# A chunked recurrence feeding two expert layers: one join product moved from TensorE to VectorE, three logits products, a Gram product placed later, and new values as sixteen wider products

## The chip, the cores and the metric

The kernel runs on one core of a Trainium2 chip. The time is the device time of one execution in microseconds (us), from the core's first to its last instruction with what lies around it. The engines are TensorE (PE; its weight loads are shown apart as PEld), VectorE (DVE), ScalarE (ACT), GpSimd (POOL) and SyncE (SP, which here only issues transfers). Each runs its own instructions in program order and waits on semaphores for the others.

## What is computed

The reference is a recurrence over 768 steps for 4 x 8 heads of 40 x 40 state, followed by a routed expert layer (8 experts, one per token) and a dense layer of 2048 hidden units:

```python
for t in range(S):
    y[:, :, t] = np.einsum('bhd,bhde->bhe', rt, state)
    Sa = np.einsum('bhde,bhe->bhd', state, at)
    state_decay = state * wt[:, :, None, :] - np.einsum('bhd,bhe->bhde', Sa, bt)
    state = state_decay + np.einsum('bhd,bhe->bhde', vt, kt)
# then x = y as (3072 tokens, 320)
expert_idx = np.argmax(x @ w_gate, axis=1)          # capacity 768 per expert
out[i] = gate_w[i] * (relu(x_i @ w1[e]) @ w2[e])
return relu(out @ w_in) ** 2 @ w_out
```

All of it is float32. The change touches the recurrence and the gate alone.

## The kernel before

The recurrence is cut into 24 chunks of 32 steps. Inside a chunk the steps depend on each other through a strictly lower triangular 32 x 32 matrix for each of the 32 heads; the kernel inverts it, so that a chunk becomes a set of small matrix products, and carries the 40 x 40 states from chunk to chunk. Four chunks' inverses are built together ("a group"): `inv_start` turns the group's matrices (`GM`) into `L` with a VectorE transpose and lists fifteen jobs, each an elementwise product into `pr` and a reduction (lines 278 and 279). Seven jobs substitute forward through 8 x 8 blocks, four (`left`, into `Xm`) and four (`right`) join pairs of 8 x 8 blocks to 16 x 16 ones. `inv_end` transposes the result into `TT` and `nat` (lines 344 and 345). The last join, of two 16 x 16 blocks to 32 x 32, is on TensorE for each chunk: `join` (32 products, line 315), a ScalarE copy to `jm` (line 318), `join_end` (32 products, line 330) and four ScalarE copies into the block matrix `TB` (`join_out`, line 340).

The loop in `run` (line 678) goes over the chunks c = 1 to 22; m is c modulo 4. All engines' order is the order of the calls. In an iteration TensorE does: `u(c)` (new values, line 442), `solve(c + 1)` (line 428), `gram(c + 7)` (line 204), `nat_k(c + 1)` with `y(c - 1)` inside it (lines 382 and 538), the gate's `logits` (line 873), `vu_t(c)` (line 504), `state(c)` (line 460), `join(c + 2)`, `scores(c)` (line 516), `nat_a(c + 2)` (line 382), `join_end(c + 2)`, in some iterations `count` (line 911), `gate.xT` (line 857) and `state_t(c + 1)` (line 487). A float32 product is two TensorE records, each a weight load and a matmul; a transpose is one. VectorE does the scans of chunk c + 8 (lines 159 and 163), the Gram mask (line 219), `gate_in` (line 547), `state_decay` (line 472 for even c, 475 for odd), the scores' mask (line 524) and, by the table `PLAN`, the inverse jobs: eight at the end of m = 0, three and fifteen (all that are left, and `inv_end`) in m = 1. ScalarE copies nearly every result out of PSUM and issues a share of the loads; GpSimd scales chunk c + 8 (`scale`, line 187) and copies the diagonal blocks (`block_T`, line 354).

PSUM tiles come from two double banks that alternate (`big`) and four single banks (`bank`): each new tile waits until the readers of the one before it in its place are done. `load_w` (line 146) brings one of the decay arrays of a chunk into the buffer `wB`, on SyncE's queue; with three buffers in turn it waits for `scale` of an earlier chunk. Ahead of the loop stands a prologue for chunks 0 to 8, written out by hand; after it come the last chunk and the expert and dense layers.

Of the kernel before, what the change touches and what calls it, by code (L numbers as in the profile page):

```python
# [35 lines left out]
class Attention:  # L36
# [8 lines left out]
    def __init__(self, tc, es, gate, zt, eb, E, VN, VR, R0, R1, x, ident):  # L45
# [45 lines left out]
        self.nat = self.natb.rearrange("p (a s) -> p a s", s=16)  # L91
        self.st, self.nb = {}, 0
# [114 lines left out]
    def gram_mask(self, c, first=True):  # L207
# [4 lines left out]
        nn = self.p2.tile([128, 2, 4, 32], F32, tag="N", name=f"N{c}", bufs=7)  # L212
# [10 lines left out]
    def inv_start(self, gi, mulengine):  # L223
# [16 lines left out]
        def left(base, xo, h, c0, c1, j0, k):  # L240
            jobs.append((gr, mulengine(k, h), ap(self.Xm, xo + c0 * h, [[h, c1 - c0], [1, h]]),
# [8 lines left out]
        for ms, h in (((0, 1), 8),):  # L250
            k = 0
            for i in range(0, h, 4):
                for g in ms:
                    st = 4 if 4 * h * (h - i) <= 640 else 2
                    for c in range(i, i + 4, st):
                        left(g * 2 * h * 33, g * 64, h, c, c + st, c, k)
                        k += 1
            gr += 1
            for i in reversed(range(0, h, 4)):
                for g in ms:  # L260
                    st = 4 if 4 * h * (i + 4) <= 640 else 2
                    for r in range(i, i + 4, st):
                        right(g * 2 * h * 33, g * 64, h, r, r + st, r + st, k)
                        k += 1
            gr += 1
        self.iv = (gi, jobs, {}, [0, 0])

    def inv(self, n):
# [5 lines left out]
        for k in range(pos[0], min(pos[0] + n, len(jobs))):  # L274
            _, _, out, in0, in1, shape = jobs[k]
            pr = self.p2.tile([128, 256], F32, tag="prod1", name=f"pr{gi}_{k}", bufs=1)
# [3 lines left out]
            pos[0] = k + 1  # L280
        if pos[0] == len(jobs):
            self.inv_end()

    def inv_blocks(self):
# [3 lines left out]
        own, other = self.GM[1].rearrange("p a b -> p (a b)"), self.natb  # L288
        prods, k, n = {}, 0, [0, 0]
        for i in range(len(jobs)):  # L290
            while k < len(jobs) and k <= i + 2 and jobs[k][0] == jobs[i][0]:
                _, eng, out, in0, in1, shape = jobs[k]
                z = eng is not V
# [13 lines left out]
    def join(self, c):  # L307

        if c >= NC:
            return  # L310
# [1394 lines left out]
```

## Time and profile before

| | us |
|---|---|
| median of 3 runs | 1085.13 (1077.47 to 1091.61) |
| the profiled execution's own time | 1090.35 |
| its span, first to last instruction | 1088.6 |
| the loop's iterations c = 1 to 16, by the first matmuls of `u` | 77.58 to 351.55 |
| the loop's iterations c = 17 to 22 | 351.55 to 439.50 |

The profile is of one execution. A row of instruction groups gives the line, the engine, the operation, the tiles, the shapes and the count, then the busy time in us and the mean duration of one in ns. "Idle before" is the time in which the engine stood still just ahead of the instruction, with what ended it; "issue" means that no wait that the profile shows ended it.

### The profile page before, as it was taken

What the parts mean: (1) busy time and instruction counts of PE and PEld (TensorE: products, weight loads), DVE (VectorE), ACT (ScalarE), POOL (GpSimd) and SP (SyncE); (2) the same over time, 40 slices, a digit from 0 to 9 for tenths busy, and PEclk for the clock granted to TensorE, in tenths of its full rate; (3) what the DMA queues carried; (4) which work ended last, traced back from release to release, by engine and by line L of the source; (5) the groups of instructions that cost most, each with busy time, mean ns of one, the idle gap of its engine ahead of it and who ended that gap; (6) DMA issues with size and microseconds to landing.
All of it is one profiled execution on the core that took longest, in us unless ns stands there. A gap on an engine that the chain in (4) does not pass through costs nothing.

```text
span 1088.6 us, 36815 instructions
## 1 busy us (share of the span) xinstructions
PE 958.5 (88%) x15578; PEld 864.7 (79%) x15578; DVE 667.5 (61%) x1368; ACT 567.1 (52%) x1342; POOL 336.6 (31%) x531
## 2 busy tenths in 40 slices
PE   5378888977888899788999998899999999999995
PEld 3367777866777888678988998789899998999995
DVE  6978566584665635747878888957534444444432
ACT  8246466565565677345655555456534343534332
POOL 5452354443554121115645555414301010000000
PEclk8588898998899889899999999899999999999998
DMA  7744655545442233274677666523100000000000
GB/s 186 184 115 145 209 156 160 160 124 177 116 138 90 66 119 101 69 200 146 190 228 216 218 213 201 166 73 105 49 25 25 25 26 25 1 25 1 26 1 27
DMA packets 80671, 123.10 MB, mean 113 GB/s; under 512 B 9679, under 2 KB 57409, under 8 KB 79561
## 3 DMA queue, kind: packets, MB, share of 16 engines
q1 hardware_dynamic: 71173, 100.09, 31.7%
q10 hardware_dynamic: 7020, 12.78, 4.1%
q0 software_dynamic: 2304, 7.78, 2.3%
q8 instruction: 124, 2.03, 0.8%
q14 instruction: 50, 0.41, 0.1%
HBM read 91.36 MB, written 29.35 MB: 111 GB/s over the span
## 4 chain that ended last, share of the span: by engine, by line
PE 71%; issue 7%; DMA 7%; DVE 7%; ACT 5%; SPq 1%; POOL 1%; ACTq 0%; DVEq 0%; POOLq 0%
PE phg L1368 16%; PE phe L1368 6%; PE pog L1394 5%; PE pog L1393 5%; PE pog L1392 5%; PE pq L516 4%; PE px L428 4%; DMA xs<-zs_s 3%; PE ps L460 3%; PE poe L1394 2%; PE poe L1392 2%; PE poe L1393 2%; DMA wB<-in_E_dram 2%; PE pa L382 2%; PE jl L315 2%
## 5 line engine op out<-in xcount | busy, mean ns | idle before, releaser
L1378 DVE SCALAR_TENSOR_TENSOR sqg<-phg,rg 128x512 f32<-128x512 f32 x96 | 66.3, 691 | 119.0 <-ACT rg L1377 119.0
L1377 ACT ACTIVATE rg<-phg 128x512 f32<-128x512 f32 x96 | 57.2, 596 | 110.4 <-PE phg L1368 110.2
L1380 DVE TENSOR_TENSOR hlg<-sqg,hhg 128x512 fp32r<-128x512 f32 x96 | 66.6, 693 | 65.9 <-ACT hhg L1379 63.2
L1379 ACT CAST hhg<-sqg 128x512 fp32r<-128x512 f32 x96 | 59.6, 620 | 78.5 <-DVE sqg L1378 78.5
L1368 PE MATMUL phg<-xhg,e 128*128 128x512 f32 x264 | 93.1, 393 | 0.0
L428 PE MATMUL px<-TB,X 128*104 128x128 f32 x384 | 60.8, 318 | 15.3 <-issue 14.1
L1394 PE MATMUL pog<-e,hlg 128*128 128x320 f32 x240 | 74.1, 309 | 0.0
L1393 PE MATMUL pog<-e,hhg 128*128 128x320 f32 x240 | 74.1, 309 | 0.0
L1392 PE MATMUL pog<-e,hhg 128*128 128x320 f32 x240 | 74.0, 308 | 0.0
L428 PEld LDWEIGHTS px<-TB,X 128*104 128x104 f32 x384 | 54.1, 203 | 17.9 <-issue 15.1
L1186 POOL TENSOR_TENSOR e<-rw,e 128x256 fp32r<-128x256 f32 x51 | 43.1, 848 | 72.2 <-ACT e L1185 69.1
L187 POOL TENSOR_TENSOR e<-e 104x512 f32<-104x512 f32 x21 | 27.9, 1327 | 121.2 <-DVE e L163 82.2
L187 POOL TENSOR_TENSOR e<-e,wB 104x512 f32<-104x512 f32 x41 | 54.0, 1337 | 35.7 <-DVE wB L159 17.1
L1507 POOL DMA_INDIRECT x2g<-zs_s,idx x24 | 23.7, 989 | 113.5 <-ACT hhg L1379 105.7
L1368 PE MATMUL phe<-xhe,e 128*128 128x480 f32 (+4 forms) x176 | 58.5, 373 | 0.0
L1368 PEld LDWEIGHTS phg<-xhg,e 128*128 128x128 f32 x264 | 49.6, 188 | 8.8
L1394 PE MATMUL poe<-e,hle 128*120 128x320 f32 (+4 forms) x150 | 47.8, 318 | 7.0 <-DVE hle L1373 7.0
L1372 ACT ACTIVATE hhe<-phe 128x480 fp32r<-128x480 f32 (+4 forms) x64 | 33.9, 530 | 36.0 <-PE phe L1368 35.7
L417 ACT ACTIVATE rhsY<-pk,sgn 64x640 f32<-64x640 f32 x48 | 38.0, 791 | 27.9 <-PE py L538 25.4
L1368 PE MATMUL phg<-xlg,e 128*128 128x512 f32 x132 | 51.7, 392 | 0.0
L354 POOL COPY TB<-TT 32x256 f32<-32x256 f32 x92 | 39.6, 430 | 39.0 <-ACT lu L431 25.3
L524 DVE TENSOR_TENSOR rq<-pq,mQ 64x512 f32<-64x512 f32 x48 | 33.0, 688 | 28.4 <-PE pq L516 28.0
(359 smaller groups left out, 2897.6 us busy)
## 6 DMA issues: line engine op xcount, KB each, us to landing
e<-in_E_dram ACTq DMA_DIRECT2D x60, 208.0 KB
rw<-in_w_dram SPq DMA_DIRECT2D x30, 320.0 KB
zs_s<-zt SPq DMA_DIRECT2D x24, 320.0 KB
rw<-in_w_dram SPq DMA_DIRECT2D x30, 256.0 KB
e<-in_E_dram SPq DMA_DIRECT2D x9, 832.0 KB
ru<-in_VR_dram SPq DMA_DIRECT2D x48, 128.0 KB
cr<-in_wi_dram SPq DMA_DIRECT2D x20, 256.0 KB
cr<-in_wo_dram SPq DMA_DIRECT2D x20, 256.0 KB
```

The costliest lines, as they stand in the source:

```text
L187: eng.tensor_tensor(z, z, f, ALU.mult)
L428: self.nc.tensor.matmul(px[par][0:104, 128 * o : 128 * o + 128], X[:, par, o, :], TB[:, 4 * par + o, :], start=True, stop=True)
L516: T.matmul(pq[s, 64 * q : 64 * q + 64], vut[:, q, s], rt[:, :, q, pp], start=True, stop=True)
L1186: (V if own else self.nc.gpsimd).tensor_tensor(W["l1"], r1, b32(W["h1"]), ALU.subtract)
L1368: T.matmul(o, lt, rt, start=(i == 0), stop=(i == len(seq) - 1))
L1377: A.activation(r[:, :n], o, AF.Relu)
L1378: V.scalar_tensor_tensor(sq[:, :n], o, 0.0, r[:, :n], ALU.max, ALU.mult)
L1379: A.copy(hh[:, :n], sq[:, :n])
L1380: V.tensor_tensor(hl[:, :n], sq[:, :n], b32(hh)[:, :n], ALU.subtract)
L1392: T.matmul(o, hh[:, t], W["h2"], start=(f == 0), stop=False)
L1393: T.matmul(o, hh[:, t], W["l2"], start=False, stop=False)
L1394: T.matmul(o, hl[:, t], W["h2"], start=False, stop=(f == NF - 1))
```

## The change

- **Join.** For groups 1 to 5 the first product of the last join is done by VectorE: six more `left` jobs of block size 16 into a new tile `Xf`, and a transpose of `Xf` into `nat` (`turn_X`). `join` with its 32 products and the copy to `jm` is left only for chunks 0 to 3; `join_end` then takes `TT` itself as its right operand. `turn_T`, the transpose into `TT`, is job 17 of 23.
- **Plan.** The jobs are spread anew: nine ahead of the loop; then four and five in m = 0, four and four in m = 1, `turn_T` alone near the start of m = 2 and five more in its middle. `inv_start` moves to the start of m = 0.
- **New values.** `u` is 16 products of 64 weight columns and 80 moving columns, in place of 32 of 32 and 40; half of what they write is not read. The result is in a double bank.
- **Logits.** Three products in place of twelve.
- **Order.** `gram` is done for chunk c + 8 after the scores of iteration c, in place of chunk c + 7 after `solve` (iteration 1 does both). `y(c - 1)` precedes `nat_k(c + 1)`; `nat_pc` and `gate.xT` precede `join_end`. `state_decay` of even c is two ScalarE copies in place of two VectorE copies.
- **Buffers.** `wB` has two buffers in place of three, `N` six in place of seven, `pr` is twice as long. `load_w` runs one chunk less ahead; in the prologue chunk 2 uses `TT`'s place, and `load_w(6)` stands behind `scale(4)`, ahead of `load(5)`, `load_v(0)` and `load_r(0)`.

```diff
     def load_w(self, c):
-        if c == 3:
-            wb = self.natb[0:104]
+        if c in (2, 3):
+            wb = self.natb[0:104] if c == 3 else self.TT.rearrange("p a b -> p (a b)")[0:104, 0:512]
         else:
-            wb = self.p2.tile([104, 512], F32, tag="wB", name=f"wB{c}", bufs=3)
+            wb = self.p2.tile([104, 512], F32, tag="wB", name=f"wB{c}", bufs=2)
...
         def left(base, xo, h, c0, c1, j0, k):
+            out = ap(self.Xm, xo + c0 * h, [[h, c1 - c0], [1, h]]) if h == 8 else ap(self.Xf, 32 * c0 + 16, [[32, c1 - c0], [1, h]])
...
+        if gi:
+            for c0, c1 in ((0, 2), (2, 4), (4, 6), (6, 8), (8, 12), (12, 16)):
+                left(0, 0, 16, c0, c1, c0 // 4 * 4, 0)
+            jobs[17:17] = [self.turn_T]
+            jobs.append(self.turn_X)
         self.iv = (gi, jobs, {}, [0, 0])
+
+    def turn_T(self):
+        self.nc.vector.transpose(self.TT.rearrange("p a j -> p j a"), self.Tt.rearrange("p t j -> p j t"))
+
+    def turn_X(self):
+        self.nc.vector.transpose(self.nat.rearrange("p a s -> p s a"), self.Xf.rearrange("p (s t) -> p s t", t=32))
...
     def join(self, c):
-        if c >= NC:
+        if c >= 4:
             return
...
-                T.matmul(p[32 * g : 32 * g + 16, 16 * k : 16 * k + 16], self.nat[s, 8 * m + k], jm[s, 16 * k : 16 * k + 16],
-                         start=True, stop=True)
+                T.matmul(p[32 * g : 32 * g + 16, 16 * k : 16 * k + 16], self.nat[s, 8 * m + k],
+                         self.TT[s, 8 * m + k, 16:32] if jm is None else jm[s, 16 * k : 16 * k + 16], start=True, stop=True)
...
     def u(self, c):
-        pu = self.bank(0, f"pu{c}")
+        pu = self.big(f"pu{c}")
         for q in range(8):
             o, qq = q // 2, q % 2
             for par in range(2):
-                for pp in range(2):
-                    g, p = 2 * qq + pp, 64 * pp + 32 * par
-                    T.matmul(pu[p : p + 32, 40 * q : 40 * q + 40],
-                             lu[:, par, o, 32 * g : 32 * g + 32], rU[:, par, q, 1 - pp, 0:40], start=True, stop=True)
+                T.matmul(pu[64 * par : 64 * par + 64, q // 4, 80 * (q % 4) : 80 * (q % 4) + 80],
+                         lu[:, par, o, 64 * qq : 64 * qq + 64], rU[:, par, q, :, 0:40], start=True, stop=True)
...
-        PLAN = (8, 3)
+        PLAN = ((4, 5), (4, 4), (5, 0), (0, 0))
...
         self.scale(4)
-        self.inv_start(0, lambda k, h: G if (h, k) in POOL else V)
+        self.load_w(6)
+        self.inv_start(0, lambda k, h: V)
         self.load(5)
         self.load_v(0)
         self.load_r(0)
         gate.init()
-        self.load_w(7)
...
-            self.load_w(c + LA + 4)
+            self.load_w(c + LA + 3)
             self.solve(c + 1)
-            self.gram(c + LA)
-            self.gram_mask(c + LA, False)
+            if c == 1:
+                self.gram(c + LA)
+                self.gram_mask(c + LA, False)
+            if m == 0 and c + 4 < NC:
+                self.inv_start(c // 4 + 1, lambda k, h: V)
+            elif m == 2:
+                self.inv(1)
             self.block_T(c + 2)
-            self.nat_k(c + 1, self.y)
+            self.y(c - 1)
+            self.nat_k(c + 1)
...
-            if m == 0 and c + 4 < NC:
-                self.inv_start(c // 4 + 1, lambda k, h: V)
-            elif m == 1:
-                self.inv(PLAN[1])
+            self.inv(PLAN[m][0])
             self.state(c)
-            self.state_decay(c, None if c % 2 else V.tensor_copy)
+            self.state_decay(c, None if c % 2 else A.copy)
...
             self.scores(c)
+            self.gram(c + LA + 1)
             self.scores_mask(c)
+            self.gram_mask(c + LA + 1, False)
...
             self.nat_a(c + 2)
+            self.nat_pc(c + 2)
+            gate.xT(c - 1)
             self.join_end(c + 2)
...
-            if m == 0:
-                self.inv(PLAN[0])
-            elif m == 1:
-                self.inv(15)
+            self.inv(PLAN[m][1])
...
-            for b in range(4):
-                s = slice(32 * b, 32 * b + 32)
-                T.matmul(pl[s, 0:8], xT[0:K, k, s], self.wg[0:K, k], start=(k == 0), stop=(k == 2))
+            T.matmul(pl[:, 0:8], xT[0:K, k], self.wg[0:K, k], start=(k == 0), stop=(k == 2))
```

## Rows read from the trace of the kernel before

**Rows 1.** The page: engines' busy time; the instruction queue (packets, MB, share).

```profile
PE 958.5 (88%) x15578; PEld 864.7 (79%) x15578; DVE 667.5 (61%) x1368; ACT 567.1 (52%) x1342; POOL 336.6 (31%) x531
q8 instruction: 124, 2.03, 0.8%
```

**Rows 2.** Busy time by stretch: length, engines' busy us (count), clock, DMA share, GB/s.

```profile
77.58:351.55 273.97, 225.75 (x8125) 201.36 (x8121) 178.70 (x331) 163.45 (x424) 122.14 (x244) 0.92 0.51 148
351.55:439.50 87.95, 78.54 (x2554) 71.46 (x2552) 46.97 (x128) 61.17 (x162) 15.24 (x25) 0.92 0.32 94
202.36:249.02 46.66, 39.40 (x1525) 34.72 (x1522) 35.73 (x63) 30.38 (x80) 26.14 (x56) 1.00 0.51 145
319.65:336.48 16.83, 13.94 (x519) 12.43 (x516) 7.25 (x15) 10.21 (x28) 7.99 (x15) 1.00 0.29 90
370.50:383.84 13.34, 12.86 (x456) 11.71 (x452) 11.47 (x28) 9.71 (x27) 4.16 (x9) 1.00 0.32 91
```

**Rows 3.** The chain that ended last, by line, within 77.58 to 351.55.

```profile
by line: issue 16.8%; PE pq L516 11.0%; PE px L428 10.7%; PE ps L460 8.3%; PE pa L382 5.0%; PE pk L382 4.9%; PE jl L315 4.8%; PE py L538 4.5%; PE jr L330 4.0%; PE pu L442 3.7%; PE G L204 3.2%; PE pv L504 3.0%; PE pn L487 2.9%; PE gpt L857 2
```

**Rows 4.** PE's timeline (start, length, count, idle before), and PE alone between two gaps.

```profile
232.01 0.45 PE L330 MATMUL jr<-jm,natb 32*16 32x16 f32 x36 [0.71 <-issue]
227.63:232.00 4.37, 3.67 (x128) 1.00 0.83 246
```

**Rows 5.** TensorE groups within 77.58 to 351.55.

```profile
L516 PE MATMUL pq<-rq,vut 128*64 128x64 f32 x512 | 31.3, 229 | 0.0
L460 PE MATMUL ps<-vu,rhsY 128*40 128x40 f32 x1024 | 25.1, 215 | 4.2 <-DVE N L219 2.2 <-issue 2.0
L442 PE MATMUL pu<-ru,lu 128*32 128x40 f32 x1025 | 14.4, 211 | 5.2 <-issue 5.2
L204 PE MATMUL G<-e 64*32 64x64 f32 (+1 forms) x1024 | 14.6, 239 | 3.4 <-DMA vu<-in_VN_dram 3.4
L315 PE MATMUL jl<-TT,GM 32*32 32x16 f32 x1024 | 14.2, 182 | 8.2 <-issue 7.8 <-ACT X L378 0.4
L873 PE MATMUL jl<-wg,gxT 128*32 128x8 f32 (+1 forms) x360 | 7.8, 182 | 0.0
L911 PE MATMUL jr<-oh,mats 128*128 128x32 f32 (+1 forms) x32 | 4.3, 275 | 0.0
```

**Rows 6.** VectorE groups by shape within 77 to 345.

```profile
L524 DVE TENSOR_TENSOR rq<-pq,mQ 64x512 f32<-64x512 f32 x30 | 20.7, 689 | 17.2 <-PE pq L516 17.0
L159 DVE TENSOR_TENSOR_SCAN wB<-wB,seeds 104x512 f32<-104x512 f32 x8 | 14.8, 1849 | 0.6
L472 DVE COPY ru<-ps 40x640 f32<-40x640 f32 x14 | 11.4, 816 | 5.9 <-PE ps L460 5.8
L163 DVE TENSOR_TENSOR_SCAN e<-e,ones 104x512 f32<-104x512 f32 x8 | 9.8, 1220 | 0.1
L344 DVE STREAM_TRANSPOSE TT<-Tt 128x1024 f32<-128x1024 f32 x4 | 8.4, 2106 | 0.4
L278 DVE TENSOR_TENSOR pr<-L,Tt 128x256 f32<-128x256 f32 x8 | 4.7, 589 | 0.1
L345 DVE STREAM_TRANSPOSE natb<-Tt 128x512 f32<-128x512 f32 x4 | 4.1, 1034 | 0.0
L279 DVE TENSOR_REDUCE Xm<-pr 128x32 f32<-128x256 f32 x8 | 3.4, 420 | 0.3
L278 DVE TENSOR_TENSOR pr<-L,Tt 128x128 f32<-128x128 f32 x8 | 3.2, 405 | 0.3
L279 DVE TENSOR_REDUCE Xm<-pr 128x32 f32<-128x128 f32 x8 | 2.3, 286 | 0.3
```

**Rows 7.** ScalarE: the state's copy (its tile's answer), and waits within 77.58 to 351.55.

```profile
L472 ACT COPY ru<-ps x2: 686/686/687, 67.7 to 68.4; 40x640 f32<-40x640 f32 x2
ACT rhsY L417 <- PE py L538: 24.0, 16, 3.7
```

**Rows 8.** SyncE's timeline in the prologue: loads of wB.

```profile
11.70 12.29 SPq L146 DMA_DIRECT2D wB<-in_E_dram  x3
```

More of the change, by code (lines that the diff above doesn't have):

```diff
@@ L248, in right @@
                          ap(Tf, base + 33 * h + r0, [[0, h], [1, r1 - r0], [32, rn]]), (h, r1 - r0, rn)))
[L250 to L265, printed above, removed]
+        for i in range(0, 8, 4):
+            for g in range(2):
+                left(g * 528, g * 64, 8, i, i + 4, i, i // 4)
+        gr += 1
+        for i in (4, 0):
+            for g in range(2):
+                right(g * 528, g * 64, 8, i, i + 4, i + 4, i // 4)
+        if gi:
[3 more added lines that the diff above has]
+            jobs.append(self.turn_X)
         self.iv = (gi, jobs, {}, [0, 0])
+    def turn_T(self):
+        self.nc.vector.transpose(self.TT.rearrange("p a j -> p j a"), self.Tt.rearrange("p t j -> p j t"))
+    def turn_X(self):
+        self.nc.vector.transpose(self.nat.rearrange("p a s -> p s a"), self.Xf.rearrange("p (s t) -> p s t", t=32))
     def inv(self, n):
@@ L274, in inv @@
         for k in range(pos[0], min(pos[0] + n, len(jobs))):
+            pos[0] = k + 1
+            if callable(jobs[k]):
+                jobs[k]()
+                continue
             _, _, out, in0, in1, shape = jobs[k]
-            pr = self.p2.tile([128, 256], F32, tag="prod1", name=f"pr{gi}_{k}", bufs=1)
+            pr = self.p2.tile([128, 512], F32, tag="prod1", name=f"pr{gi}_{k}", bufs=1)
             pv = pr[:, 0 : int(np.prod(shape))].rearrange("p (a b c) -> p a b c", a=shape[0], b=shape[1], c=shape[2])
@@ L279, in inv, with inv_blocks @@
             V.tensor_reduce(out, pv, axis=AX.X, op=ALU.add)
[L280 to L284, printed above, removed]
+    def inv_blocks(self, engines):
         gi, jobs, _, _ = self.iv
         V = self.nc.vector
-        own, other = self.GM[1].rearrange("p a b -> p (a b)"), self.natb
+        own, other = self.TT.rearrange("p a b -> p (a b)"), self.natb
         prods, k, n = {}, 0, [0, 0]
@@ L291, in inv_blocks @@
             while k < len(jobs) and k <= i + 2 and jobs[k][0] == jobs[i][0]:
-                _, eng, out, in0, in1, shape = jobs[k]
-                z = eng is not V
+                _, _, out, in0, in1, shape = jobs[k]
+                z = k in engines
                 pr = (other[:, 256 * (n[1] % 2) :] if z else own[:, 256 * (n[0] % 4) :])[:, 0 : int(np.prod(shape))]
@@ L300, in inv_blocks @@
             V.tensor_reduce(jobs[i][2], prods.pop(i), axis=AX.X, op=ALU.add)
-        self.inv_end()
+        self.turn_T()
+        V.transpose(self.nat.rearrange("p a s -> p s a"), self.Tt[:, 0:16])
+        self.iv = None
     def shared(self, c):
@@ L314, in join @@
                 s = slice(32 * g, 32 * g + 32)
-                T.matmul(p[s, 16 * k : 16 * k + 16], self.GM[c // 4 % 2][s, 8 * m + k], self.TT[s, 8 * m + k, 16:32],
+                T.matmul(p[s, 16 * k : 16 * k + 16], self.GM[0][s, 8 * m + k], self.TT[s, 8 * m + k, 16:32],
                          start=True, stop=True)
@@ L627, in run @@
         self.scale(5, (V, G, V))
-        self.load_w(8)
+        self.load_w(7)
         self.solve(0)
@@ L635, in run @@
         self.scale(6, (V, G, V))
-        self.load_w(9)
+        self.load_w(8)
         self.gram_mask(5)
@@ L650, in run @@
         self.scale(7, (V, G, G))
-        self.load_w(10)
+        self.load_w(9)
         self.scan(8)
@@ L664, in run @@
         self.load(9, 3)
-        self.load_w(11)
+        self.load_w(10)
         self.load_v(2)
@@ L730, in run @@
             self.join_out(c + 2)
-            gate.xT(c - 1)
-            self.nat_pc(c + 2)
             self.state_t(c + 1)
```

27 lines of the change are left out of this document (12 added, 15 removed).

## The prediction

> **What bounds the kernel now.** I began with the page: TensorE is busy for 88% of the span, but this hides that the change touches only the recurrence, the first 440 us [rows 1]. So I cut the loop at the first matmul of `u` and asked for busy time by stretch [rows 2]. Iterations 1 to 16 take 273.97 us, 17.1 each; in them TensorE is busy for 225.75 and VectorE for 178.70. TensorE stands still for 48.2 us. The chain of waits says what these are: its largest single part, 16.8% of the stretch or 46 us, is "issue", time in which nothing that the profile shows held the engine [rows 3]. The timeline gives it a shape. Before the second part of `join_end` stands a gap of 0.71 us, and from the end of the gap before it exactly 128 matmuls ran, in 4.37 us of which 3.67 were busy [rows 4]. The instruction queue moved 124 packets in 2.03 MB, 16.4 KB each; TensorE's 15578 matmuls and 15578 weight loads divided by 124 packets give 251 instructions in a packet, so 128 matmuls with their loads are one packet [rows 1]. The gaps are TensorE waiting for its next packet of instructions. An iteration has 8125 / 16 = 508 matmuls, 3.97 packets, and 46 us over 63.5 packets is 0.72 us for each. What TensorE pays for is thus the number of instructions as well as their work.
>
> The Trainium skill (Runtime: NRT & Kernel Launch, section Instruction fetch mechanics) says that instructions come in 16 KiB blocks of 256, which agrees with the packets, and that crossing a block is mostly hidden, which the gap of 0.71 us does not show. By its second half the count of instructions would be free; that is a rival below.
>
> Without such gaps an iteration is shorter: number 18 has none and takes 13.34 us, with 456 matmuls, without a Gram product and with the eight records of `count` [rows 2].
>
> **The change, part by part, for iterations 1 to 16.**
>
> *TensorE's instructions.* `join` goes: 64 records. `u` goes from 64 to 32, the logits from 24 to 6. Of 508 records 394 are left, 3.08 packets. At 4.37 us for a packet that is 13.5 us, less than the iteration below, so I take the gaps as gone, where they were 46 / 16 = 2.9 us an iteration; if each packet left still cost 0.72 us, they would be 2.2.
>
> *TensorE's work.* `join` gave 14.2 / 16 = 0.89 us [rows 5]. Six logits records of 128 weight columns: like those of `count`, 4.3 / 32 = 0.134 us each, 0.81 in place of 24 x 0.0217 = 0.52; plus 0.3. The new `u` has no row. It alternates the halves of the output partitions, as `state` does (25.1 / 1024 = 0.0245 us a record); its 64 weight columns are those of `scores` (31.3 / 512 = 0.061). So 32 records cost 0.78 to 1.96 us, against 64 x 0.0140 = 0.90 now [rows 5]. I take 1.3, nearer to the row that alternates, with something for twice as many moving columns: plus 0.4. The Trainium skill (TensorEngine Tiling (Array Packing), section Key Properties) lets different tiles work at once; four narrow tiles before and two wide ones after, each with twice the columns, would by it make `u` twice as long, an estimate of 1.8 us, and the sum 8 us worse over the sixteen.
>
> *What is late next.* With the gaps gone the scores wait for ScalarE, which copies `u`, the state's transpose, `lu`, `rhsY` and `vut` in one chain behind `u`; TensorE's time under this chain (`join`, the logits) is hidden, the longer `u` is not. `y` ahead of `nat_k` takes away a wait of `rhsY` for `y` that was 24.0 us in 16 iterations [rows 7], but ScalarE then waits for the transposes instead, so I take nothing for it. The Gram product, 14.6 / 16 = 0.9 us [rows 5], now stands behind the scores, where nothing hides it. So an iteration without `count` is 13.34 - 8 x 0.134 + 0.9 + 0.4 = 13.6 us, one with it 14.6. The even `state_decay` on ScalarE (2 x 0.686 us, [rows 7]) comes after `vut` and ahead of work that waits for the Gram product, so it costs nothing there.
>
> *VectorE.* A job of n elements is a product and a reduction: 0.405 + 0.286 us for 128, 0.589 + 0.420 for 256 [rows 6], or 0.375 + 0.00248 n. The six new ones have 512, 512, 384, 384, 512 and 256: 8.6 us in a group of four iterations (in proportion to the 256 form, 10.1, the upper bound). `turn_X` replaces a transpose of its size. The even copies (4 x 0.816) leave. Per group 178.70 / 4 = 44.7 becomes 50.0 us, 12.5 an iteration: less than 13.6, but unevenly spread. The late Gram product adds a wait: `state_t` takes the bank of the Gram product, so it stands behind VectorE's scores' mask and Gram mask (2 x 0.689 + 0.4 = 1.8), and `u(c + 1)` stands behind it. Undisturbed, 3.8 us of TensorE work follow the scores (Gram 0.9, `nat_a` 0.9, `gate.xT` 0.5, `join_end` 0.8, `state_t` 0.7), and the masks end 2.0 before the iteration does, 1.3 before they would delay it. From the masks of m = 0 on VectorE has no pause. Five jobs (100, 144, 196, 256, 256): 4.2. In m = 1 the scans with their small operations 3.5 (1.85 + 1.22 + 0.4), `gate_in` 0.5, four jobs 3.4, `state_decay` 1.64, masks 1.8: they end 13.0 into m = 1, on time. Four jobs (128, 128, 512, 512) 4.7; in m = 2 scans 3.5, `turn_T` 2.1, `gate_in` 0.5, four jobs and `turn_X` 6.3, masks 1.8: 18.2 into m = 2 (with m = 1 at 13.7), and with `state_t` the iteration takes 18.9. A group is 13.6 + 13.7 + 18.9 + 14.6 = 60.8 us.
>
> *Against the present.* Iterations 8 to 10 and 15, one of each m at a clock of 1.00, make 46.66 + 16.83 = 63.5 us; the mean of all groups is 273.97 / 4 = 68.5, at a mean granted clock of 0.92, a mixture of its two levels of 2.4 and 1.2 GHz [rows 2]. These 5.0 us of half clock and transfers I take as 3.5 afterwards (bounds 0 and 5.0: fewer gaps, but a pause in m = 2). Then 64.3, and 4.2 x 4 = 17 us less.
>
> *Iterations 17 to 22.* Now 87.95 us. Without Gram product or scans VectorE is no bound: 13.34 + 0.4 with `count`, 12.7 without, so 79 and 2 for the clock: 7 us less (bounds 3 and 9).
>
> *Buffers and the prologue.* In the loop `load_w` waits for the same `scale` as before and its array is needed more than an iteration later: nothing (an array that landed over 16 us late would show). In the prologue SyncE already stands for 12.29 us over three loads of `wB` [rows 8]; now `load_w(6)` waits for `scale(4)` with `load(5)`, `load_v(0)` and `load_r(0)` behind it, and each later array goes one place down, so `scan(7)` may wait. I take a loss of 2 us (bounds 0, as the loads in the queue cover it, and 6).
>
> *Sum.* 17 + 7 - 2 = 22 us less than the profiled execution's 1090.35, so 1068. This execution is 5.2 above the median of the runs, so the prediction is 1063.
>
> **Rivals.**
>
> *VectorE absorbs the rest.* If the new products run well below the fit, or the Gram mask isn't what `state_t` waits for, m = 2 is 13.6 too: a group of 55.4 and 3.0 for the clock, 10 us less, 40 in all, 45 with the rest: 1040. For it: VectorE's 50.0 us fit. Against: its order. Chance 0.2.
>
> *The gaps don't go with the instructions.* Then only the work counts: 0.2 us an iteration on TensorE, while m = 2 gets longer by some 3 us a group: about 1085, no change. This is the skill's rule on blocks at its word. The 128 matmuls between gaps speak against it. Chance 0.12.
>
> *VectorE's share stays.* VectorE now works 44.7 of 68.5 us, 65%; the rest is waiting in program order. If its share stays there, a group of 50.0 us of work takes 77, 8.4 more: 34 - 7 + 2 us worse, 1114. It decides from a share under 67%. Against it: in iterations 8 to 10 the share is 35.73 / 46.66 = 77%. Chance 0.1.
>
> **How the numbers follow.** My own case has 0.5, with 1050 to 1078 for its unknown sizes (`u`, the clock, the prologue); the remaining 0.08 is a mixture that ends within 2%. A measurement of this kernel can tell about 2% from no change, 1063.4 or less. Of my case a little over half lies under that: 0.28, with the first rival 0.48 for faster; slower 0.12, for the third rival and a prologue gone wrong; the same 0.40. The range reaches into the first rival and over the second: 1038 to 1088.
>
> **What would show it.** Right: matmuls of an iteration near 394, "issue" under a third of its share, m = 2 the longest iteration with TensorE standing before `state_t` or `join_end` behind VectorE, and ScalarE's `vut` ahead of the scores. Wrong: gaps as many as packets and as long as now; `u` over 1.6 us; `scan` waiting for `wB`; or a loop in which all four m are alike, which would put VectorE's jobs off the path.

## The result, and the profile after

| | before | after |
|---|---|---|
| median, us | 1083.32 (1075.63 to 1093.28, 14 runs) | 1072.18 (1067.98 to 1076.66, 14 runs) |
| ratio | | 0.9898, 95% interval 0.9866 to 0.993 |
| the profiled execution's own time | 1090.35 | 1068.04 |
| iterations 1 to 16 | 273.97 | 251.40 |
| iterations 17 to 22 | 87.9 | 82.67 |
| start to `u(1)` | 77.58 | 81.76 |
| `u(23)` to the experts' first transpose | 20.5 | 27.8 |
| from there to the end | 628.6 | 622.6 |

The change is about 1% faster. The interval lies wholly below 1, so the gain is clear of noise, but it is under 2%; the time is inside the predicted range. The page of the changed kernel, busy time, the instruction queue and the chain by engine:

```profile
PE 953.6 (89%) x13098; PEld 865.7 (81%) x13098; DVE 693.5 (65%) x1407; ACT 574.1 (54%) x1344; POOL 342.0 (32%) x531
...
q8 instruction: 105, 1.72, 0.7%
...
PE 57%; DVE 18%; DMA 8%; ACT 7%; issue 6%; POOL 2%; SPq 1%; ACTq 0%; DVEq 0%; POOLq 0%
```

TensorE has 2480 matmuls fewer, and 19 packets fewer come [rows 1]; that is 261 instructions (a matmul and its load are two) for each. The work by stretch, first the two loop stretches, then one group's iterations m = 1, 2, 3 and 0 (busy time by engine, granted clock, DMA share, GB/s):

```profile
core 0: us, PE busy (x) PEld busy (x) DVE busy (x) ACT busy (x) POOL busy (x), PEclk, DMA share, GB/s
81.76:333.16 251.40, 219.24 (x6378) 199.75 (x6379) 202.07 (x367) 167.81 (x422) 125.05 (x237) 0.94 0.55 161
333.16:415.83 82.67, 74.94 (x1930) 69.46 (x1926) 48.85 (x131) 63.07 (x162) 17.89 (x32) 0.96 0.34 99
148.73:165.22 16.49, 13.40 (x397) 12.01 (x393) 15.71 (x28) 10.23 (x27) 9.46 (x20) 0.96 0.54 147
165.22:181.74 16.52, 15.16 (x396) 14.01 (x394) 15.99 (x24) 11.31 (x28) 6.44 (x8) 0.83 0.48 135
181.74:197.38 15.64, 13.72 (x405) 12.56 (x401) 9.27 (x22) 9.10 (x24) 5.29 (x7) 1.00 0.58 159
197.38:211.54 14.16, 12.63 (x396) 11.52 (x393) 9.34 (x21) 10.81 (x28) 8.78 (x23) 1.00 0.52 145
```

VectorE fills m = 1 and m = 2 (15.71 of 16.49 us, 15.99 of 16.52) and is idle for a third or more of the other two. What TensorE waits for in both loop stretches (total us, times, longest):

```profile
PE pk L384 <- ACT rhsY L496: 7.4, 14, 0.6
PE jr L338 <- DVE natb L271: 7.2, 4, 3.6
PE pa L384 <- DVE ru L476: 6.9, 5, 2.0
PE pq L517 <- ACT vut L508: 6.4, 19, 0.4
PE pn L488 <- DVE N L221: 3.0, 3, 1.0
PE jr L338 <- issue: 2.9, 5, 1.1
```

Before, this view was led by "issue" (iterations 1 to 16):

```profile
PE px L428 <- issue: 14.1, 10, 2.5
PE jl L315 <- issue: 7.8, 10, 1.7
PE jr L330 <- issue: 5.8, 9, 1.3
```

To see what replaced it I added up TensorE's idle times over 0.02 us within iterations 1 to 16, by what ended them; the last column is what remains of the stretch. The rows below the second are runs of the experiments.

| kernel | matmuls per iteration | us | issue | ScalarE | VectorE | other | granted clock | running |
|---|---|---|---|---|---|---|---|---|
| before | 508 | 274.0 | 40.1 | 2.5 | 2.2 | 3.4 | 0.92 | 225.8 |
| after | 399 | 251.4 | 6.5 | 11.7 | 15.1 | 0 | 0.94 | 218.1 |
| few_instr | 459 | 296.5 | 18.1 | 23.5 | 0.6 | 0 | 0.87 | 254.3 |
| few_early | 459 | 275.2 | 19.7 | 21.5 | 0.9 | 0 | 0.94 | 233.1 |
| join_back | 459 | 264.1 | 26.0 | 4.9 | 1.4 | 0 | 0.94 | 231.8 |
| u_narrow | 431 | 259.7 | 18.0 | 7.6 | 14.7 | 0.5 | 0.91 | 218.9 |
| plan | 399 | 245.3 | 2.6 | 15.6 | 12.5 | 1.9 | 0.97 | 212.7 |
| best2 | 399 | 259.4 | 4.0 | 10.2 | 16.5 | 4.6 | 0.92 | 224.1 |
| final | 399 | 245.5 | 4.0 | 15.1 | 9.7 | 0 | 0.95 | 216.7 |

From before to after the gaps give 33.6 us, the running time 7.7 and a transfer's wait 3.4; new waits for VectorE take back 12.9 and for ScalarE 9.2. That is the 22.6 us of the stretch. A second trace of the changed kernel (base_after) has 252.1 us in this stretch and 83.3 in iterations 17 to 22, so its loop repeats to 1 us; of the kernel before there is one trace.

That the gaps are waits for the next packet of instructions, as the prediction inferred, the trace's record of packets shows. Before, 38 of the gaps called "issue" in iterations 1 to 16 were longer than 0.2 us, and all 38 ended 1.19 to 1.60 us after a packet of the instruction queue had landed, while such packets came every 4.0 us.

### The profile page after: what moved, and what is told of

It reads as the page before. It is cut to its first block, busy times and chain, and to the rows that moved or that the text cites. A ratio compares the mean times of both kernels' runs of the same rounds, so it can differ in the third digit from the quotient of the medians.

```text
span 1066.2 us, 31888 instructions
## 1 busy us (share of the span) xinstructions
PE 953.6 (89%) x13098; PEld 865.7 (81%) x13098; DVE 693.5 (65%) x1407; ACT 574.1 (54%) x1344; POOL 342.0 (32%) x531
## 4 chain that ended last, share of the span: by engine, by line
PE 57%; DVE 18%; DMA 8%; ACT 7%; issue 6%; POOL 2%; SPq 1%; ACTq 0%; DVEq 0%; POOLq 0%
PE phg L1368 16%; PE pog L1394 5%; PE pog L1393 5%; PE pog L1392 5%; PE phe L1368 4%; DVE pr L287 3%; PE pq L517 3%; PE pu L442 2%; DMA wB<-in_E_dram 2%; ACT vu L448 2%; PE px L430 2%; POOL ct L1106 2%; DMA wof_s<-ct 1%; PE pk L384 1%; PE poe L1394 1%
## 5 line engine op out<-in xcount | busy, mean ns | idle before, releaser
L430 PE MATMUL px<-TB,X 128*104 128x128 f32 x384 | 55.4, 305 | 1.3 <-ACT TB L348 1.3
L448 ACT COPY vu<-pu 32x320 f32<-32x320 f32 x96 | 40.0, 417 | 29.0 <-PE pu L442 28.2
L517 PE MATMUL pq<-rq,vut 128*64 128x64 f32 x768 | 47.5, 230 | 7.4 <-ACT vut L508 6.4
L430 PEld LDWEIGHTS px<-TB,X 128*104 128x104 f32 x384 | 50.4, 194 | 4.0 <-ACT TB L348 1.4
L517 PEld LDWEIGHTS pq<-rq,vut 128*64 128x64 f32 x768 | 44.1, 143 | 11.0 <-ACT vut L508 9.8
L356 POOL COPY TB<-TT 32x256 f32<-32x256 f32 x92 | 41.9, 455 | 31.9 <-DVE TT L268 15.0
```

The source lines that it names most:

```text
L430: self.nc.tensor.matmul(px[par][0:104, 128 * o : 128 * o + 128], X[:, par, o, :], TB[:, 4 * par + o, :], start=True, stop=True)
L448: A.copy(vu[64 * pp : 64 * pp + 32, pp, :, par].rearrange("p (h q) d -> p h q d", h=2), v)
L517: T.matmul(pq[s, 64 * q : 64 * q + 64], vut[:, q, s], rt[:, :, q, pp], start=True, stop=True)
```

## The experiments

Four questions: does the number of records cost time apart from their work; why isn't fewer records alone a gain; was the join worth moving; and what would mend the new waits. Ratios are to the kernel before on the same chip. The edits are shortened: names and arguments are cut, a comment names the run, and small changes that an edit brings with it are left out.

**1. Records against work.** Products that nobody reads stand before the scores of each iteration, once as 32 narrow products (64 records), once as three wide ones (6 records) of about the same TensorE time (0.86 and 1.00 us busy an iteration in their traces).

```diff
+            for k in range(8):            # more_narrow
+                for g in range(4):
+                    s = slice(32 * g, 32 * g + 32)
+                    T.matmul(st["jl"][s, 256 + 16 * k : 272 + 16 * k], ident[s, s], ident[s, 0:16], ...)
+            for k in range(3):            # more_wide
+                T.matmul(st["jl"][:, 256 + 16 * k : 272 + 16 * k], ident, ident[:, 0:16], ...)
             self.scores(c)
```

> The kernel before with 32 more narrow products an iteration (32 x 32 weights from the identity, 16 columns, never read) ahead of the scores: 64 records, 0.8 us of TensorE work by join's rows. Theory 'instructions': half a packet more, 0.5 x 4.37 = 2.2 us an iteration, 35 to 48 us over the loop. Theory 'work': 0.8 x 22 = 18 us, or nothing where TensorE waits for ScalarE there.

> The same place with 3 wide products (128 x 128 weights, 16 columns, never read): 6 records, about the same 0.8 us of work. Theory 'instructions': 0.05 packets, 0.2 us; the work lies partly in gaps: 0 to 8 us over the loop, far less than the narrow ones. Theory 'work': as the narrow ones, 18 us.

Measured: narrow 1148.65 us, ratio 1.0499 (1.0445 to 1.0553), 58 us above the kernel before and so more than either theory allowed; wide 1112.53, ratio 1.0147 (1.0076 to 1.0219), 22 us above it, near the 18 of the theory "work" and not the 0 to 8 of the other. Both also wait 0.4 us an iteration for the copy `jm`, which reads the same bank, a flaw that is the same in both. Their difference, 36 us, is 1.6 us in each of 22 iterations for 58 records: about the same work costs more as many narrow records than as few wide ones, by 3.6 us for 128. That is far more than the 0.72 us of a gap. In the narrow run's trace the gaps grew from 40.1 to 46.0 us only, while the granted clock fell from 0.92 to 0.83 and the running time rose from 225.8 to 262.1. Of these 36 us the added products are 14; the rest goes with the lower clock. Whole executions agree: the granted clock was 0.904 to 0.919 in the four narrow ones, and 0.926 to 0.942 in the three quicker wide ones and in the kernel before on that chip. So a part of the price is the clock and not the gaps. How the 36 us between the two runs divide I can't say, since the wide run's profiled execution lay 8 us above its median; nor was it tried whether it is the number of the narrow products or their size that goes with the lower clock.

**2. Fewer records alone.** The kernel before with the wide `u` in a double bank and three logits products, first in its own order, then with the copies of `Pn` and `gxT` ahead of `join_end`, where the changed kernel has them.

```diff
-        pu = self.bank(0, f"pu{c}")          # few_instr and few_early
+        pu = self.big(f"pu{c}")              # and 16 products for 32, 3 logits products for 12
             self.nat_a(c + 2)
+            self.nat_pc(c + 2)               # few_early only
+            gate.xT(c - 1)
             self.join_end(c + 2)
             self.join_out(c + 2)
-            gate.xT(c - 1)
-            self.nat_pc(c + 2)
```

> The kernel before with two parts of the change alone: new values as 16 wide products (in a double bank) and three logits products. TensorE has 508 - 32 - 18 = 458 records an iteration, but more work: the wide products take 1.26 us from start to start in the changed kernel's trace, the narrow ones 0.73, the logits 0.3 us more; 0.8 us in all. Theory 'instructions' (TensorE waits for packets of 128 matmuls with their loads, 4.37 us each at least): 3.58 packets in place of 3.97, 1.7 us less an iteration for the packets, so the time falls in spite of the work, by 0.3 to 1.0 us an iteration or 5 to 16 us over the loop. Theory 'work' (the gaps are something else and stay): 0.8 x 22 = 17 us longer.

> The kernel before with the new values as 16 wide products, three logits products, and ScalarE's copies of Pn and gxT moved ahead of the wait for the join's second step, as the changed kernel has them. The same edit without the move took 1,124 us against 1,091, and its trace shows the new values waiting for the copy of Pn 16 times, 18.1 us in all, since they now take their bank behind it. Theory that this new wait ate the gain of the 50 missing records: the wait goes, and the time falls by 18 to 30 us, to 1,094 to 1,106, in its trace no wait of pu for Pn above 0.2 us. Theory that the wide products themselves are the loss (0.5 us more of TensorE in each iteration and a lower granted clock): it stays at 1,112 or above.

Measured: few_instr 1124.48, ratio 1.0268 (1.0197 to 1.0338), slower than either theory allowed; few_early 1089.13, ratio 1.0012 (0.9968 to 1.0056), the kernel before's time and 35 us under few_instr, more than the 18 to 30 expected. What TensorE waits for longest in iterations 1 to 16 of few_instr, and then of few_early:

```profile
PE pu L440 <- ACT Pn L403: 18.1, 16, 2.3
```

```profile
PE G L204 <- ACT rhsY L494: 17.3, 15, 1.3
```

The double bank brought these waits. In it `u` stands behind the tile whose last reader is the copy of `Pn`, late in ScalarE's order; with that copy moved, the Gram product behind `u` stands behind `state_c`'s copy into `rhsY`, for up to 1.3 us an iteration. In both the gaps fell by half (40.1 to 18.1 and 19.7), and a wait of the same size took their place. What makes few_instr slower, and not only even, is its running time: 254.3 us for 225.8, of which the wider products are 13 (0.8 us an iteration, an estimate from their rows) and the rest goes with a granted clock of 0.87. In the changed kernel the Gram product stands behind the scores, and the wait for `rhsY` is 7.4 us in 14 times, the first row of the view of after; that this move took it away was not tried by itself.

**3. The join, and the new values.** The changed kernel with the join on TensorE for all chunks, and with 32 narrow products in `u` again.

```diff
-        if c >= 4:                           # join_back
+        if c >= NC:
             return
-            for c0, c1 in ((0, 2), ...): left(0, 0, 16, ...)
-        PLAN = ((4, 5), (4, 4), (5, 0), (0, 0))
+        PLAN = ((4, 5), (4, 2), (1, 0), (0, 0))
-        pu = self.big(f"pu{c}")              # u_narrow, with its 32 products
+        pu = self.bank(0, f"pu{c}")
```

> The changed kernel itself, unaltered, as the yardstick on the same chip for the other kernels of this group. Every theory expects what was measured of it: a ratio to the kernel before of 0.987 to 0.993, some 1,070 to 1,080 us.

> The changed kernel with the first join step on TensorE again in every chunk (64 records and one ScalarE copy more in each of 19 iterations, ten VectorE instructions fewer in a group of four). Theory that the records are what counts: 64 products at about 0.69 us, and half a packet at 0.35 to 1.9 us, in 19 iterations are +20 to +49 us, less at most 12 us that the lighter VectorE gives back in the second and third iteration of each group: 1,080 to 1,110. Theory that VectorE is what bounds the changed kernel, so that moving the join to it was no gain: those two iterations fall from 17.0 to about 14.5 us, and the whole to 1,055 to 1,070.

> The changed kernel with the 32 narrow products of the new values back (single bank). 426 records an iteration in place of 394 (3.33 packets; at 4.0 us each 13.3 us, still under the iteration of 14). Theory 'chain' (with the gaps gone, u leads ScalarE's chain to the scores, so its length counts): 0.5 us less in every iteration that VectorE does not set, some 5 to 10 us less than the changed kernel, ratio to the kernel before about 0.98 to 0.985. Theory 'instructions still count': gaps come back, 0.2 to 0.7 us an iteration, ratio 0.99 to 1.0.

Measured: base_after, the changed kernel again, 1072.47, ratio 0.9874 (0.9814 to 0.9934); join_back 1076.03 on the same chip, ratio 0.9893 (0.9832 to 0.9953). The intervals overlap, and 1076 lies between the two theories' ranges: the join moved to VectorE is worth little or nothing. The trace shows both theories at work. Iterations 1 to 16 take 264.1 us, 12 more than base_after's 252.1. About 10 of these are running time, which now holds the 64 products of each chunk; "issue" is 19.5 us longer, and the waits for VectorE and ScalarE are 17 shorter. Iterations 17 to 22 take 77.9, 5.4 less: `jr` in iteration 18 no longer waits for VectorE. In 1 to 16 the lighter VectorE does not shorten m = 1 and m = 2 (17.06 and 16.79 us on average, after 17.21 and 16.79), although the waits for VectorE are 1.4 us in place of 15.1: 26.0 us of issue, for 6.5, stand where they stood.

join_back can also be set beside few_early, on the same chip: both have 459 matmuls an iteration, the wide `u`, three logits products and the join on TensorE. What join_back has besides is the changed kernel's order (the Gram product behind the scores, `y` ahead of `nat_k`, the even `state_decay` on ScalarE, the inverse jobs spread over m = 0 to 2) and its buffers. It takes 1076.0 us for 1089.1, ratio 0.9893 for 1.0012, with intervals that do not overlap. So at this number of records the new order with its buffers is worth 13 us, about as much as the whole change. No run has the new order with the 508 matmuls of before, and none the three logits products by themselves.

u_narrow gave 1070.96, ratio 0.9805 (0.9758 to 0.9851), in the range of the theory "chain"; its interval lies below the changed kernel's first one (0.9866 to 0.993) and overlaps the second (base_after), and its time is the changed kernel's within 2 us. In its trace the gaps are back, as the other theory said (18.0 us for 6.5), and its loop takes 259.7 us for 251.4. So the wide `u` by itself is neither a gain nor a loss that these runs could tell.

**4. VectorE's order.** The same work for VectorE, with its 23 jobs spread otherwise.

```diff
-            jobs[17:17] = [self.turn_T]
-            jobs.append(self.turn_X)
+            jobs += [self.turn_T, self.turn_X]
-        PLAN = ((4, 5), (4, 4), (5, 0), (0, 0))
+        PLAN = ((8, 6), (1, 3), (5, 0), (0, 0))      # plan
+        PLAN = ((5, 5), (2, 2), (2, 0), (0, 7))      # best2, a group begun at the end of m = 3
```

In both, `block_T` in m = 2 stands behind VectorE's jobs, and the single job near the start of m = 2 goes. best2 has the two edits of the run ends (experiment 5) as well: these are "the same two edits" of its expectation.

> The changed kernel with the same work, but VectorE's twelve solve steps and six join products spread over the four iterations of a group in another way: fourteen of them in the iteration with the least other VectorE work, four in the next, five in the third. Theory that VectorE's backlog sets the second and third iteration of a group (17.2 and 16.8 us against 13.7 and 15.1): they fall to about 14 to 15 us, the first rises to about 14.5, so that four groups lose 4 to 5 us each and the whole falls by 12 to 20 us, to 1,050 to 1,060. Theory that TensorE's own work and its clock set them and VectorE is only busy beside it: no change within 5 us of the changed kernel on this chip.

> The same two edits, and VectorE's solve started one iteration earlier, at the end of the fourth iteration of a group, in which VectorE had only 10 us of work: 7 of its 23 steps there, 10 in the first, 4 in the second and 3 in the third, its two transposes among these. Theory that VectorE's place in the order, not its amount of work (53 us in a group of 60), made the second and third iteration long: all four come to 13.5 to 15 us, with the waits for natb and for state_decay's ru gone; iterations 1 to 16 take 228 to 240 us (251 in the changed kernel) and the whole 1,045 to 1,055. Theory that VectorE's amount of work is the bound: another iteration of the group grows in their place, and the time is that of the run named ends, within 4 us.

Measured: plan 1065.14, ratio 0.9802 (0.9745 to 0.9858), beside base_after's 0.9874: 7 us less, about half of the gain that was expected. The two intervals overlap, but all four executions of plan (1063.0 to 1069.7) lie below all four of base_after (1070.5 to 1078.6). A group of it, m = 1, 2, 3 and 0:

```profile
151.02:165.15 14.13, 12.54 (x397) 11.46 (x394) 13.52 (x23) 9.15 (x23) 7.39 (x15) 1.00 0.44 124
165.15:181.05 15.90, 12.68 (x393) 11.46 (x393) 15.47 (x22) 12.30 (x33) 9.10 (x14) 1.00 0.67 183
181.05:195.51 14.46, 13.53 (x406) 12.44 (x402) 10.43 (x21) 9.21 (x24) 5.30 (x7) 1.00 0.67 170
195.51:209.52 14.01, 12.71 (x397) 11.52 (x393) 12.57 (x25) 10.50 (x26) 8.84 (x22) 1.00 0.58 152
```

In this group m = 1 fell by over 2 us, to the length TensorE needs; m = 2 stays at 15.9, VectorE busy for 15.47 of it. The waits left there are `jr` for `natb` (1.4 us) and `pn` for the Gram mask (1.0). In after the same iteration took 16.5 us with 1.0 us of such waits, at a granted clock of 0.83 in place of 1.00. best2 gave 1062.77, ratio 0.984 (0.98 to 0.988). Its own yardstick is ends on the same chip (1066.98, 0.988): 4 us less, so the theory of VectorE's place, which said 1,045 to 1,055, failed, and the other came near. Its profiled execution, the longest of six, had 259.4 us in iterations 1 to 16 (said 228 to 240). A group of it, m = 2, 3, 0 and 1:

```profile
168.23:182.86 14.63, 14.29 (x395) 13.28 (x393) 8.71 (x14) 10.55 (x26) 6.57 (x9) 0.86 0.64 169
182.86:200.15 17.29, 15.27 (x406) 14.15 (x402) 10.05 (x19) 10.05 (x28) 5.27 (x7) 0.90 0.53 150
200.15:216.18 16.03, 12.61 (x397) 11.46 (x393) 15.06 (x35) 11.05 (x28) 8.12 (x16) 1.00 0.44 124
216.18:233.85 17.67, 15.47 (x398) 14.11 (x394) 16.93 (x27) 10.26 (x27) 12.49 (x29) 0.80 0.57 160
```

Here m = 2 is relieved (8.71 us of VectorE) and m = 0 and 1 are full: the seven jobs that I put at the end of m = 3 stand behind its Gram mask, and so ran in m = 0. VectorE's free time in m = 3 lies ahead of that mask, where the group's matrix is not yet complete. Its 50 us a group are under the group's length, but neither order spreads them evenly. The gain in the last group shows (17 to 22 in 78.3 us for plan's 82.8).

**5. Prologue and tail, and all together.**

```diff
-        if c in (2, 3):                      # prologue: wB of chunk 6 in Xf's place,
+        if c in (2, 3, 6):                   # the later loads one place earlier
-        pl = ... if c < NC - 3 else self.at.big(f"pl{c}")[:, 0]
+        pl = ... if c < NC - 3 else self.at.bank(0, f"pl{c}")
-            self.inv(PLAN[m][0])             # final, besides plan's table
+            self.inv({1: 5, 16: 9, 17: 3}.get(c, PLAN[m][0]))
-            self.inv(PLAN[m][1])
+            self.inv({1: 4, 16: 8}.get(c, PLAN[m][1]))
```

> The changed kernel with the two stretches mended that my sum had mis-sized, and nothing else: in the prologue the load of wB for chunk 6 goes into Xf's place, which is cleared later, so that the loads for chunks 6 to 8 are issued one place earlier, as in the kernel before (the changed one waited 5.8 us for one at the scan of chunk 7); in the last iteration the logits of chunks 21 to 23 take the bank of pu's old place, not one behind the copy of pn (3.2 us of wait at 417 us, and the granted clock at its lower level behind it). Theory that these two waits are the 11 us which the prologue and the tail lost: 1,060 to 1,067, 6 to 11 us under the changed kernel's 1,072, with the first new values of iteration 1 at 77 to 80 us, and 20 to 24 us from the last new values to the first product of the experts. Theory that other work (the clock, queues of transfers) takes their place: 1,069 to 1,074.

> The run named best2 with the new values as 32 narrow products in one bank again (0.73 us of TensorE for 1.26, but 32 more matmuls and weight loads in each of 24 iterations, a quarter of a packet). Theory that TensorE's own work is what is left in front: 0.5 us less in 22 iterations, 6 to 12 us faster than best2. Theory that the packets are: a quarter of a packet at the 3.8 us that the runs with 64 narrow and 6 wide extra products differ by is 0.95 us in each iteration, so 0.4 us net in 22 iterations, 5 to 12 us slower. The same edit on the changed kernel gave 1,071 beside the changed one's 1,072, which told neither.

> The plan run's order of VectorE's solve, in the last group started earlier (17 of its 23 steps in iteration 16, 6 in iteration 17, so that its transposes end before iteration 18), and the two edits of the run named ends in prologue and tail. Theory that the three waits are separate prices: the plan is worth what it measured (0.7 per cent), the wait of 3.9 us for natb in iteration 18 goes with the lower clock behind it (17 to 22 from 82.8 to 76 to 79 us), and the tail gives 3 us: ratio 0.970 to 0.978 to the kernel before, and 1,049 to 1,056 us in the profiled execution. Theory that each wait mended only uncovers the next (as the earlier start of the solve did in every group): the ratio is that of the plan run, 0.980, or above.

Measured: ends 1066.98, ratio 0.988 (0.9837 to 0.9924), not to be told from the changed kernel. The tail's wait went and its 27.8 us became 24.3, for the 20 to 24 expected. In the prologue the edit did what it was meant to: the array of chunk 7 was issued at 39.59 us in place of 53.62, and its scan no longer waits. The scan's instruction in after, then in ends:

```profile
66.48 0.18 DVE L171 TENSOR_TENSOR Pc<-wB,e 104x16 f32<-104x16 f32 x1 [5.81 <-DMA wB<-in_E_dram]
```

```profile
62.08 0.18 DVE L170 TENSOR_TENSOR Pc<-wB,e 104x16 f32<-104x16 f32 x1
```

But `u(1)` comes only 0.6 us sooner, at 81.1 for the 77 to 80 expected. Of TensorE's waits from 40 us to `u(1)` these two differ most from after's, where the first is not there and the second is 5.9 us:

```profile
PE pn L487 <- ACT GM L222: 3.0, 1, 3.0
PE jl L322 <- issue: 1.6, 2, 0.9
```

and what ScalarE waited for in it from 60 to 81 us, with the transfers that it issued just before:

```profile
ACT X L378 <- DMA wB<-in_E_dram: 5.4, 1, 5.4
```

```profile
72.84 5.61 ACTq L138 DMA_DIRECT2D e<-in_E_dram  x4
```

This is another wait of the same length, for another array. ScalarE issues the four loads of chunk 9 ahead of the copy into `X`, and the last of them stood until a load of `wB` had landed: that of chunk 10, issued at 73.12. In after the four took 2.57 us. So one wait was mended and the next one uncovered. The 1,067 is at the edge of the first theory's range, but the kernel before was quicker on that chip too (1080.6), and the ratio shows no gain.

best2_narrow gave 1066.66, ratio 0.9869 (0.9825 to 0.9913), against best2's 0.984; its iterations 1 to 16 took 259.4 us as best2's did. So the narrow `u` is neither of the two theories' 5 to 12 us; with experiment 3 it may be called even.

final gave 1059.33, ratio 0.9762 (0.9683 to 0.9842), the fastest of all and as its first theory said (0.970 to 0.978; the profiled execution 1055 for 1049 to 1056); its interval lies below the changed kernel's first one (0.9866 to 0.993) and touches the second (base_after). Its two loop stretches:

```profile
80.84:326.29 245.45, 217.44 (x6379) 198.24 (x6379) 206.24 (x377) 167.25 (x422) 128.37 (x236) 0.95 0.56 163
326.29:403.67 77.38, 72.16 (x1929) 66.58 (x1926) 45.07 (x121) 62.95 (x162) 18.25 (x34) 1.00 0.37 106
```

The three parts did add up, in the profiled executions against after: 6 us in 1 to 16, 5.3 in 17 to 22 (no wait for `natb` in iteration 18), 5.3 in the tail.

## Why the prediction was right, and where it was not

**The sum.** I said 22 us less than the profiled execution of before; the profiled execution of after has 22.3 less. By stretches: minus 22.6 (said 17), minus 5.2 (7), plus 4.2 (2), plus 7.2 and minus 6.0 (both not in the sum). It fits because the errors cancel: that the sum came out to the microsecond is luck.

**The step from sum to median** is what made 1063 of 1072. I carried over that before's profiled execution was above its median (by 7.0 with all runs); after's own is 4.1 below its median. Of the 22 us between the two profiled executions 11 are such scatter, as much as the effect: the medians differ by 11.1, half of what I said. Of it 6 us may be the unchanged expert and dense layers, which took 622.4 to 628.6 us in the profiled executions; for the rest of it the other executions have no trace, so it stays open.

**Gaps and packets: right.** An ordinary iteration has 393 matmuls, 401 with `count` (said 394), TensorE's "issue" went from 40.1 to 6.5 us, and the fewer matmuls a kernel has the less of it there is (508, 459, 431 and 399 in the table, with scatter). The sign that I named, a third of the chain's share, failed: it went from 16.8% [rows 3] to 9.8%.

```profile
by line: DVE pr L287 13.5%; issue 9.8%; PE pu L442 5.5%; PE pq L517 5.3%; ACT vu L448 4.0%; DVE rq L525 4.0%; ACT rhsY L419 3.7%; DVE Tt L288 3.6%; PE pk L384 3.3%; DVE Xf L288 3.3%; DVE ru L476 3.1%; DVE wB L161 3.0%; PE pn L488 2.8%; DVE 
```

The chain now runs through VectorE's jobs and ScalarE's copies, and time ahead of their instructions counts as issue too: of the 24.6 us only 3.6 stand ahead of a TensorE instruction, before 38.9 of 46.2. A share of a chain is not the share of one cause. By the rule of the Trainium skill that I weighed (Runtime: NRT & Kernel Launch, Instruction fetch mechanics), blocks are mostly hidden; the traces disagree for this stream, with 40.1 us of gaps in 16 iterations of 508 matmuls, the longer ones all just behind the landing of a packet.

**TensorE's work: right in size.** The new `u` in a clean iteration of after, start to start 1.26 us (before 0.73): plus 0.53 for the 0.4 that I took, and well under the other estimate of 1.8 us. The third row is `scores` behind ScalarE, as foreseen.

```profile
197.38 1.33 PE L442 MATMUL pu<-ru,lu 128*64 128x80 f32 x32
198.64 1.99 PE L430 MATMUL px<-TB,X 128*104 128x128 f32 x16
...
205.69 1.90 PE L517 MATMUL pq<-rq,vut 128*64 128x64 f32 x32 [0.33 <-ACT vut L508]
```

The iterations that VectorE does not hold take 13.72 (m = 0, said 13.6) and 15.13 us (m = 3, said 14.6). What the step left out is that `u` changes its bank, and with it who waits for whom: in experiment 2 the waits that this brought were as long as the gaps that went. I counted the move of the Gram product as a small price and that of `nat_pc` not at all; with both, and with the rest of the new order, these waits are mostly gone (experiment 3).

**VectorE: right in amount, wrong in place.** 50.5 us a group (202.07 / 4) for 50.0. But I had m = 1 on time at 13.7 and m = 2 at 18.9; they are 17.21 and 16.79, together 34.0 for 32.6. So the sign "m = 2 the longest iteration" did not come. The step that failed is "they end 13.0 into m = 1, on time": in iteration 5 the masks ended 14.7 us into it, for a reason told in the last section, and the wait comes one bank earlier, at `pa`, which takes the double bank that `state_decay` still reads (6.9 us in 5 waits). With the clock in it a group takes 62.9 us, for my 64.3. In m = 2 it is `natb` and the Gram mask, as I said, with 1.0 us for the mask.

**Iterations 17 to 22.** "VectorE is no bound" failed in one of six: `jr` waits 3.6 us for `natb` in iteration 18, the last group's final job. final removed it and got 77.4 us, for my 81.

**Prologue and tail.** The prologue's wait came as said, with twice the size but within its bounds: `scan(7)` stood 5.8 us for `wB`. The tail I had not looked at: its logits take a double bank, which now lies behind `state_c`'s reading of `pn`:

```profile
420.36 1.54 PE L873 MATMUL pl<-wg,gxT 128*128 128x8 f32 x6 [3.20 <-ACT rhsY L496]
```

The wait is under half of the 7.2 us. The rest goes with the clock, which was granted at 0.92 in the tail before and 0.64 after:

```profile
439.47:460.00 20.53, 14.54 (x358) 12.21 (x355) 14.95 (x81) 6.35 (x22) 2.96 (x3) 0.92 0.24 61
415.83:443.60 27.77, 22.45 (x272) 19.70 (x268) 13.44 (x77) 6.55 (x21) 3.93 (x4) 0.64 0.21 56
```

In ends, without the wait, it was still 0.66; why, no run shows. A tile that is put into a rotating pair shifts its neighbours wherever the pair is used, also in code that the diff doesn't show.

**The rivals.** VectorE's share came to 202.07 / 251.40 = 80%, so the third is out; the gaps went, so the second is out; the first is what plan and final go toward, and even they leave 10 to 13 us of waits for VectorE.

## What to carry to other kernels

Where a stream of small matmuls shows regular gaps that nothing ends, count instructions: their number is a cost beside their work. But fewer records pay only if nothing else stands in the place of the gaps: here the wide `u`, half of which is thrown away, and the join on VectorE were each about even when taken back, and the new order at the same number of records was worth 13 us. So list first, for each tile that changes its bank, which reader it will stand behind. And when a cost goes to an engine that has room on average, write down in which iteration it has this room; a forecast from one profiled execution is no better than the scatter between executions.

## What the hardware showed that was not expected

VectorE's elementwise products slow down beside GpSimd's work, the small ones most. The products of `L` and `Tt` in iterations 1 to 16 (count, busy us, mean ns), before and then after:

```profile
L278 DVE TENSOR_TENSOR pr<-L,Tt 128x128 f32<-128x128 f32 x8 | 3.2, 405 | 0.3
...
L278 DVE TENSOR_TENSOR pr<-L,Tt 128x16 f32<-128x16 f32 x5 | 0.9, 175 | 0.2
```

```profile
L287 DVE TENSOR_TENSOR pr<-L,Tt 128x512 f32<-128x512 f32 x12 | 8.7, 723 | 0.4
...
L287 DVE TENSOR_TENSOR pr<-L,Tt 128x128 f32<-128x128 f32 x8 | 8.3, 1036 | 0.1
...
L287 DVE TENSOR_TENSOR pr<-L,Tt 128x16 f32<-128x16 f32 x5 | 2.5, 510 | 0.2
```

Those of 128 elements take longer than those of 512. One of them in iteration 5 of after, and what GpSimd did:

```profile
154.70 1.20 DVE L287 TENSOR_TENSOR pr<-L,Tt 128x128 f32<-128x128 f32 x1
```

```profile
154.48 2.55 POOL L189 TENSOR_TENSOR e<-e,wB 104x512 f32<-104x512 f32 x2 [1.16 <-DVE wB L161]
156.98 2.09 POOL L356 COPY TB<-TT 32x256 f32<-32x256 f32 x4
```

Two products of one form in the run plan, and what GpSimd did beside the second, while it did nothing beside the first:

```profile
212.83 0.39 DVE L286 TENSOR_TENSOR pr<-Xm,Tt 128x128 f32<-128x128 f32 x1
...
217.47 1.27 DVE L286 TENSOR_TENSOR pr<-Xm,Tt 128x128 f32<-128x128 f32 x1
```

```profile
217.24 2.65 POOL L189 TENSOR_TENSOR e<-e,wB 104x512 f32<-104x512 f32 x2 [1.16 <-DVE wB L161]
```

The long ones run beside `scale`, the short one doesn't. This holds for iterations 1 to 16 of all fourteen traces: products of `L` and `Tt` of 128 elements took 273 to 292 ns with GpSimd idle beside them (10 of them) and 888 ns on average beside `scale` (64); those of 512 took 691 to 693 (30) and 1049 to 1061 (10). The reductions keep their length (0.28 and 0.29 us), beside `scale` too. The new plan puts the small products beside `scale`, and that is where VectorE's delay in m = 1 comes from: the four jobs there took 5.3 us in iteration 5 for my 3.4, and the masks were 1.7 late. My line was drawn through rows of before of which some had run beside GpSimd's work (the 0.589 us for 256 elements is 0.425 without it), so the longer products came out under it (1.41 us with the reduction for 512 elements, for 1.64), and the total still agreed. No run was made to try GpSimd's part by itself, but plan put other products beside `scale`, and then those were the long ones.
